# A layer-norm's inverse root seeded by one ScalarE operation, and its scaled tables built on GpSimd, ahead of a spectral filter and a GLU block

## The chip, the cores and the metric

The kernel runs on one core of a Trainium2 chip. The metric is device time of one execution in microseconds, as the median over runs of the same program. The core has a matrix engine (PE, TensorE; its weight loads are listed as PEld), VectorE (DVE), ScalarE (ACT), GpSimd (POOL), and SyncE (SP), whose queue issues most of the transfers.

## The reference

All tensors are fp32. S = 2048 rows, D = 640 columns, F = 1728.

```python
x = A_x                                            # (1, 2048, 640)
n = (x - mean(x, -1)) / sqrt(var(x, -1) + 1e-5)    # layer norm without weights
X = rfft2(n, axes=(-2, -1)) * (w_r + 1j * w_i)
h = x + irfft2(X, s=(S, D))
m = (h - mean(h, -1)) / sqrt(var(h, -1) + 1e-5)
out = h + ((m @ w_gate) * (m @ w_up)) @ w_down
```

## The kernel before, in words

Both transforms are written as matrix products. The 2048 rows are taken as 16 tiles of 128 rows (`NT = 16`; tile t holds every sixteenth row from t on), each in a buffer `x` of 128 partitions and 640 columns. The program has a first stage that takes the tiles one after the other, a second stage over 16 groups of frequencies (filter), the way back, a second norm, and then the GLU block, which takes some three quarters of the time. The order on every engine is the order in which the code records the operations; each engine works its own list in that order and waits on semaphores for what others produce.

**The first stage, a tile t.** The norm is never written out. Its mean goes into the folding, its scale into a table:

- *Statistics.* For some tiles DVE computes them (two `bn_stats` halves and a `bn_aggr`: lines 176, 179, 180, result `mv`), for others ACT (an `Identity` pass that sums the row, line 195, and a `Square` pass that sums the squares into `sq`, line 196). `m2` is twice the mean (line 182), `ve` the variance plus epsilon (lines 183 and 198).
- *Inverse root* (`inverse_root`, lines 205 to 209). ACT takes the square root `sd` of `ve`, DVE its reciprocal `r`, and three small DVE operations (`w`, `w`, `r`) make one Newton step. This is done in groups of tiles: 0, 1, (2,3), (4,5), (6 to 9), (10,11), (12,13), (14,15).
- *Scaled table* (`scale_c`, lines 267 and 269). `CR[t]` is a 128 x 128 table `cct` whose rows are multiplied by `r`. It lies in one of four buffers (in `bits`). The list `SCALE_ON_ACT` says which engine makes it: ACT for tiles 0 and 5 to 15, DVE for tiles 1 to 4.
- *Folding* into one of four buffers `fold`: `odd` (line 229, on DVE, or on POOL for the tiles named in `FOLDS` and for tile 0) is a two-input subtraction of 320 columns; `even` is a two-input operation with the mean (line 234, 322 columns) and two further two-input sums (lines 238 and 239, 64 and 320 columns).
- *Product* (`s1_mm`, line 252): seven matrix products against `CR[t]`, each run as two fp32 passes, 14 passes a tile. The first four products need only the results of lines 234 and 229, the last three also those of lines 238 and 239.
- ACT copies the results out of PSUM (`s1_main`, line 278, and `s1_rest`, line 275).

On POOL, ahead of the `odd` of another tile, stands a one-element copy `hold` (line 360) that reads the last folding of the tile before: it keeps POOL from starting earlier.

`weave` and the list in `GROUPS` put the small operations of the inverse root between the big ones on DVE. `scale_shift` uses the same `moments` and `inverse_root` for the second norm, in four groups.

Of the kernel before, what the change touches and what calls it, by code (L numbers as in the profile page):

```python
# [37 lines left out]
SCALE_ON_ACT = (0, *range(AHEAD, NT))  # L38
# [40 lines left out]
def tile_spectral_glu(ctx: ExitStack, tc: tile.TileContext, x, wre, wim, wgu, wlast, wdown, wdlast,  # L79
                      cc, ci, fmain, frem, imain, irem, mm, out):  # L80
    nc = tc.nc

    keep = ctx.enter_context(tc.tile_pool(name="keep", bufs=1))
    work = ctx.enter_context(tc.tile_pool(name="work", bufs=8))
    small = ctx.enter_context(tc.tile_pool(name="small", bufs=5))
# [3 lines left out]
    tt, act = nc.vector.tensor_tensor, nc.scalar.activation  # L89
# [10 lines left out]
    def bank(tag, bufs=2):  # L100
        return pools["y" if tag in ("im2", "ir2") else "a"].tile([P, 512], F32, tag=tag, name=tag, bufs=bufs)
# [28 lines left out]
    cct = keep.tile([P, P], F32, name="cct")  # L130
# [34 lines left out]
    def moments(ts, junk=None, total=None, k=0):  # L165
        n = len(ts)
        m2 = small.tile([P, n], F32, tag="m2", name="m2")
        ve = small.tile([P, n], F32, tag="ve", name="ve")

        def statistics(ts):  # L170
            n = len(ts)
            mv = small.tile([P, n, 2], F32, tag="mv", name="mv")
            fs, late = [], None
            for i, t in enumerate(ts):
                st = small.tile([P, 2, 6], F32, tag="st", name="st")
                fs.append(lambda st=st, t=t: nc.vector.bn_stats(st[:, 0], X[t][:, 0:320]))
                if late:
                    fs.append(late)
                fs.append(lambda st=st, t=t: nc.vector.bn_stats(st[:, 1], X[t][:, 320:640]))
                late = lambda st=st, i=i: nc.vector.bn_aggr(mv[:, i], st)  # L180
            fs.append(late)
            fs.append(lambda: nc.vector.tensor_scalar(m2[:, 0:n], mv[:, :, 0], 2.0, None, op0=OP.mult))
            fs.append(lambda: nc.vector.tensor_scalar(ve[:, 0:n], mv[:, :, 1], EPS, None, op0=OP.add))
            return fs

        if junk is None:
            return m2, ve, statistics(ts)
        first = statistics(ts[:k]) if k else []
        sq = small.tile([P, n], F32, tag="sq", name="sq")
        fs = []  # L190
        if total is not None:
            fs.append(lambda: nc.vector.tensor_scalar(m2, total, 2.0 / D, None, op0=OP.mult))
        for i, t in list(enumerate(ts))[k:]:
            if total is None:
                fs.append(lambda t=t, i=i: act(junk[i], X[t], AF.Identity, scale=2.0 / D, accum_out=m2[:, i:i + 1]))
            fs.append(lambda t=t, i=i: act(junk[i], X[t], AF.Square, bias=m2[:, i:i + 1], scale=-2.0,
                                           accum_out=sq[:, i:i + 1]))
        fs.append(lambda: nc.vector.tensor_scalar(ve[:, k:n], sq[:, k:n], 0.25 / D, EPS, op0=OP.mult, op1=OP.add))
        return m2, ve, first + fs

    def inverse_root(ve, r, n):
        sd = small.tile([P, n], F32, tag="sd", name="sd")
        w = small.tile([P, n], F32, tag="w", name="w")
        return [
            lambda: act(sd, ve, AF.Sqrt),
            lambda: nc.vector.reciprocal(r, sd),
            lambda: nc.vector.scalar_tensor_tensor(w, r, -0.5, r, op0=OP.mult, op1=OP.mult),  # L207
            lambda: tt(w, w, ve, op=OP.mult),
            lambda: nc.vector.scalar_tensor_tensor(r, w, 1.5, r, op0=OP.add, op1=OP.mult),
        ]  # L210

    SC = {}

    def front(ts, k):
        n = len(ts)
        r = small.tile([P, n], F32, tag="r", name="r")
        junk = [fold[:, o:o + D] for o in (NR * 1026, NR * 1026 + D)]
        m2, ve, fs = moments(ts, junk * 2 if k < n else None, k=k)
        for i, t in enumerate(ts):
            SC[t] = r[:, i:i + 1], m2[:, i:i + 1]  # L220
        return fs, inverse_root(ve, r, n)

    def folded(t):
        o = t % NR * 1026
# [18 lines left out]
    PS1, CR = {}, {}  # L243
# [19 lines left out]

    def scale_c(t):
        CR[t] = crs[t % 4]
        if t in SCALE_ON_ACT:
            act(CR[t], cct, AF.Copy, scale=SC[t][0])
        else:
            nc.vector.tensor_scalar(CR[t], cct, SC[t][0], None, op0=OP.mult)

    def at(base, t):
        return view(base, 4 * t, [[64, 32], [1, 4]])
# [17 lines left out]

    warm = wk([P, P], "warm")
    nc.vector.memset(warm, 0.0)
    pw = bank("re")
    for n in range(16):
        nc.tensor.matmul(pw[:, 0:P], warm, warm, start=True, stop=True)
    f0, c0 = front((0,), 1)
    f1, c1 = front((1,), 0)
    for f in f0:
        f()
    for ts, when, aside, root in GROUPS:  # L300
        k = len(when)
        fs, cs = front(ts, k)
# [15 lines left out]
    for t in range(NT):  # L318
        if t == 1:
            nc.gpsimd.dma_start(frall, frem)  # L320
        if t >= 1:
            fs = even(t)
            if t + 1 < NT and t + 1 not in ASIDE:
                fs.insert(1, (0.4, lambda: odd(t + 1, nc.vector)))
            if t < AHEAD:
                fs.insert(1 + (t <= 2), (0.2, lambda: scale_c(t)))
            if t == 1:
                fs, (recip, w, *left) = fs[1:], dve[1][0]
                for f in (c1[4], fs[0][1], fs[1][1], recip, fs[2][1], w):
# [24 lines left out]
        else:  # L354
            e0 = [f for _, f in even(0)]
            c0[0]()
            for f in (e0[0], c0[1], e0[1], c0[2], c0[3], e0[2], c0[4], *f1[:-1]):
                f()
        if t in FOLDS:
            nc.gpsimd.tensor_copy(small.tile([P, 1], F32, tag="hold", name="hold"), folded(t)[1][:, 383:384])  # L360
            for k in FOLDS[t]:
                odd(k, nc.gpsimd)
        if t >= 1:
            for f in stats[t]:
                f()
            if AHEAD <= t + 1 < NT and t + 1 not in SCALE_ON_ACT:
                scale_c(t + 1)
        else:
            scale_c(0)
# [378 lines left out]
    def scale_shift(ts, junk, total=None):  # L748
        n = len(ts)
        r = small.tile([P, n], F32, tag="r", name="r")  # L750
        b = small.tile([P, n], F32, tag="b", name="b")
        m2, ve, fs = moments(ts, junk, total)
        cs = inverse_root(ve, r, n)
# [105 lines left out]
    total = small.tile([P, 8], F32, tag="total", name="total", bufs=1)  # L859
# [310 lines left out]
    for n, (blk, p) in enumerate(steps):  # L1170
        if p == 6:
# [356 lines left out]
```

## Time and profile before

| | us |
|---|---|
| runs of the kernel | 674.58, 674.81, 676.47; median 674.81 |
| the profiled execution | 675.71, of which the span of the program 673.9 |
| PE busy in the span | 662.8 (98%) |
| DVE busy in the span | 471.3 (70%) |
| first product of the first stage starts | 8.97 after the span's start |
| first product of the second stage starts | 38.92 |
| PE waiting in between, by the window from 8.97 to 38.87 | 2.6 (27.29 busy of 29.90) |

Busy times of a whole span are averages over stages with different limits. A row of the timeline reads: start, duration, engine, line, operation, output<-inputs, shape, count, and in brackets how long the engine had been idle and what by the profile ended that. Rows of one engine overlap by some 0.08 us, since the next operation is set up while the last one drains.

### The profile page before, as it was taken

The numbers are of one execution on the slowest core, as the hardware profiler recorded it, in microseconds if no ns is written. First come the engines' busy times: TensorE is split into PE (matmuls) and PEld (weight loads), VectorE is DVE, ScalarE is ACT, GpSimd is POOL, SyncE is SP. The second block draws the span as 40 slices with busy tenths as digits, with TensorE's granted clock in tenths as the row PEclk, the third lists the DMA queues.
The fourth block names the chain that finished last, engine by engine and source line by source line (L and its number), as shares of the span: only waits on it lengthen the run. The fifth ranks groups of instructions, "written<-read, shape, count | busy, mean of one in ns | idle before, by whom it ended". The sixth has DMA issues, their size and how long they took to land.

```text
span 673.9 us, 10264 instructions
## 1 busy us (share of the span) xinstructions
PE 662.8 (98%) x3695; PEld 588.0 (87%) x3695; DVE 471.3 (70%) x967; ACT 322.7 (48%) x622; POOL 393.0 (58%) x377
## 2 busy tenths in 40 slices
PE   7999999999999999999999999999999999999997
PEld 6999898887898888888888899898888888888887
DVE  6969896788767868584858657754747575756654
ACT  6977674585624244362626246534434252525220
POOL 3101124650298887878787544188787878787610
PEclk9999999999999999999999999999999999999999
DMA  8638975502212110042342458212002121212004
GB/s 317 225 103 258 268 223 157 179 6 78 79 40 78 40 59 25 36 115 63 92 84 79 98 116 274 79 40 68 16 34 79 40 78 40 79 40 80 1 1 156
DMA packets 48953, 66.12 MB, mean 98 GB/s; under 512 B 24082, under 2 KB 30670, under 8 KB 48774
## 3 DMA queue, kind: packets, MB, share of 16 engines
q1 hardware_dynamic: 48246, 62.91, 30.6%
q0 software_dynamic: 288, 2.16, 0.8%
q8 instruction: 29, 0.48, 0.3%
q10 hardware_dynamic: 368, 0.39, 0.3%
q14 instruction: 22, 0.18, 0.1%
HBM read 54.61 MB, written 10.84 MB: 97 GB/s over the span
## 4 chain that ended last, share of the span: by engine, by line
PE 92%; DMA 4%; DVE 2%; issue 1%; ACT 1%; SPq 0%; DVEq 0%; ACTq 0%
PE e L119 49%; PE d L119 26%; PE eo L119 4%; PE re L119 2%; PE u L455 2%; PE y L119 2%; PE im L119 2%; PE im L507 2%; DMA x<-in_x_dram 2%; PE im L252 1%; DMA bits<-in_mm_dram 1%; PE ir L507 1%; DMA wts<-in_wre_dram 1%; PE y L773 0%; SPq L155 0%
## 5 line engine op out<-in xcount | busy, mean ns | idle before, releaser
L119 PE MATMUL e<-xt,wst 128*128 128x512 f32 x864 | 213.2, 391 | 0.0
L119 PEld LDWEIGHTS e<-xt,wst 128*128 128x128 f32 x864 | 159.9, 188 | 30.5
L1047 DVE TENSOR_TENSOR x<-d,x 128x320 f32<-128x320 f32 x280 | 123.3, 483 | 51.6 <-PE d L119 47.6
L119 PE MATMUL d<-wd,ht 128*128 128x320 f32 x832 | 143.6, 309 | 0.0
L119 PEld LDWEIGHTS d<-wd,ht 128*128 128x128 f32 x832 | 131.2, 188 | 7.6
L961 POOL TENSOR_TENSOR wst<-raw,wst 128x1024 fp32r<-128x1024 f32 x23 | 55.4, 2409 | 67.2 <-ACT wst L960 49.2
L119 PE MATMUL e<-t,wst 128*128 128x512 f32 x360 | 94.4, 392 | 0.0
L119 PEld LDWEIGHTS e<-t,wst 128*128 128x128 f32 x360 | 66.3, 188 | 12.6
L119 PE MATMUL d<-wt,ht 128*128 128x320 f32 x360 | 69.5, 310 | 0.0
L977 POOL TENSOR_TENSOR wst<-raw,wst 128x896 fp32r<-128x896 f32 (+1 forms) x46 | 65.1, 1438 | 0.2 <-ACT wst L972 0.2
L119 PEld LDWEIGHTS d<-wt,ht 128*128 128x128 f32 x360 | 57.3, 188 | 2.3
L1063 ACT ACTIVATE ht<-e 128x512 fp32r<-128x512 f32 x44 | 26.4, 599 | 51.5 <-DVE e L1126 25.9
L1102 ACT ACTIVATE h<-e 128x512 f32<-128x512 f32 x24 | 14.3, 595 | 67.3 <-PE e L119 67.3
L1022 DVE TENSOR_TENSOR x<-d,x 128x320 f32<-128x320 f32 x62 | 27.5, 485 | 23.4 <-PE d L119 23.4
L658 ACT ACTIVATE wd<-draw 128x320 fp32r<-128x320 f32 (+1 forms) x30 | 15.7, 558 | 57.4 <-POOL draw L668 54.3
L972 ACT ACTIVATE wst<-raw 128x896 fp32r<-128x896 f32 (+1 forms) x48 | 30.2, 677 | 26.6 <-POOL raw L966 25.8
L119 PE MATMUL e<-xt,wdir 128*128 128x512 f32 x180 | 41.9, 392 | 0.4 <-DVE w L207 0.2
L119 PEld LDWEIGHTS e<-xt,wdir 128*128 128x128 f32 x180 | 33.5, 188 | 8.1 <-ACT xt L783 0.7
L1122 DVE TENSOR_TENSOR e<-e,h 128x512 f32<-128x512 f32 x24 | 16.8, 698 | 30.8 <-PE e L119 17.7
L1066 DVE TENSOR_TENSOR ht<-e,ht 128x512 fp32r<-128x512 f32 x54 | 36.9, 685 | 1.6 <-ACT ht L1063 1.3
L637 POOL TENSOR_TENSOR wd<-draw,wd 128x640 fp32r<-128x640 f32 x8 | 12.4, 1576 | 40.5 <-ACT wd L636 40.5
L1119 ACT ACTIVATE h<-e 128x512 f32<-128x512 f32 x24 | 14.3, 597 | 40.1 <-PE e L119 40.1
(234 smaller groups left out, 1189.5 us busy)
## 6 DMA issues: line engine op xcount, KB each, us to landing
raw<-in_wgu_dram SPq DMA_DIRECT2D x24, 640.0 KB
draw<-in_wdown_dram SPq DMA_DIRECT2D x24, 320.0 KB
wts<-in_wre_dram SPq DMA_DIRECT2D x16, 322.0 KB
x<-in_x_dram SPq DMA_DIRECT2D x15, 320.5 KB
out_dram<-x SPq DMA_DIRECT2D x15, 320.0 KB
bits<-in_mm_dram SPq DMA_DIRECT2D x32, 128.0 KB
wts<-in_wim_dram SPq DMA_DIRECT2D x9, 322.0 KB
zfar<-zr SPq DMA_DIRECT2D x32, 80.0 KB
```

The lines of the kernel that those rows point to most:

```text
L119: nc.tensor.matmul(o, l, r, start=start, stop=stop, skip_group_check=True)
L507: nc.tensor.matmul(out, y[:, h, a:b], inv(g, h), start=n == 0, stop=n == len(ys) - 1)
L658: act(o[:, 0, a:a + n], src, AF.Copy)
L961: ptt(wa[:, 1], stage[:, 0:1024], f32(wa[:, 0]), op=OP.subtract)
L972: act(ws[:, 0, o:o + b - a], stage[:, a:b], AF.Copy)
L977: ptt(ws[:, 1, o:o + b - a], stage[:, a:b], f32(ws[:, 0, o:o + b - a]), op=OP.subtract)
L1022: tt(xv, ps[b][:, 0:320], xv, op=OP.add)
L1047: tt(xv, o, xv, op=OP.add)
L1063: act(hop[:, a, 0], src, AF.Copy)
L1066: engine.tensor_tensor(hop[:, a, 1], src, f32(hop[:, a, 0]), op=OP.subtract)
L1102: act(h0, oa, AF.Copy)
L1122: tt(ob, ob, h1, op=OP.add)
```

## The change

Four things are changed in the first stage, and the first of them in the second norm too, which calls the same functions.

1. The square root on ACT and the reciprocal on DVE become one ACT operation, `Abs_reciprocal_sqrt`, whose result is the seed `r`. Where a group's variance comes from one engine alone, it reads the variance `mv` or the sums `sq` directly, with epsilon as a bias (a new 128 x 1 constant `eps`), and where it comes from `bn_aggr` alone, the addition of epsilon (`ve`) goes too: the Newton step adds it itself.
2. The scaled tables of tiles 3 to 15 are made by POOL: eleven leave ACT, two (tiles 3 and 4) leave DVE. Tiles 1 and 2 stay on DVE, tile 0 on ACT. On POOL a table stands where `t` is one less than its tile, ahead of the `hold` and `odd` of that `t`.
3. Tile 0's table stands between the two passes of tile 1's statistics on ACT, where it stood behind both.
4. On DVE, the last folding of tile 0 (line 239) stands behind the end of tile 0's Newton step, where it stood ahead of it.

The diff, without the second norm's call sites:

```diff
-        return m2, ve, statistics(ts)
-        first = statistics(ts[:k]) if k else []
+            fs = statistics(ts, True)
+            var = spread_of["mv"]
+            return m2, (var, 1.0, lambda w: nc.vector.scalar_tensor_tensor(w, var, EPS, w, op0=OP.add, op1=OP.mult)), fs
+        first = statistics(ts[:k], False) if k else []
...
-        return m2, ve, first + fs
+        times = lambda w: tt(w, w, ve, op=OP.mult)
+        return m2, ((ve, None, times) if k else (sq, 0.25 / D, times)), first + fs
...
-    def inverse_root(ve, r, n):
-        sd = small.tile([P, n], F32, tag="sd", name="sd")
+    def inverse_root(spread, r, n):
+        src, scale, times = spread
         w = small.tile([P, n], F32, tag="w", name="w")
+        root = AF.Abs_reciprocal_sqrt
         return [
-            lambda: act(sd, ve, AF.Sqrt),
-            lambda: nc.vector.reciprocal(r, sd),
+            lambda: act(r, src, root) if scale is None else act(r, src, root, bias=eps, scale=scale),
+            lambda: None,
             lambda: nc.vector.scalar_tensor_tensor(w, r, -0.5, r, op0=OP.mult, op1=OP.mult),
-            lambda: tt(w, w, ve, op=OP.mult),
+            lambda: times(w),
             lambda: nc.vector.scalar_tensor_tensor(r, w, 1.5, r, op0=OP.add, op1=OP.mult),
         ]
...
     def scale_c(t):
         CR[t] = crs[t % 4]
-        if t in SCALE_ON_ACT:
+        if t == 0:
             act(CR[t], cct, AF.Copy, scale=SC[t][0])
         else:
-            nc.vector.tensor_scalar(CR[t], cct, SC[t][0], None, op0=OP.mult)
+            (nc.vector if t < 3 else nc.gpsimd).tensor_scalar(CR[t], cct, SC[t][0], None, op0=OP.mult)
...
+    eps = keep.tile([P, 1], F32, name="eps")
+    nc.vector.memset(eps, EPS)
...
-            if t < AHEAD:
+            if t < 3:
                 fs.insert(1 + (t <= 2), (0.2, lambda: scale_c(t)))
...
-                if t + 1 in SCALE_ON_ACT:
-                    scale_c(t + 1)
...
-            for f in (e0[0], c0[1], e0[1], c0[2], c0[3], e0[2], c0[4], *f1[:-1]):
+            for f in (e0[0], c0[2], e0[1], f1[0], c0[3], c0[4]):
                 f()
+            scale_c(0)
+            for f in (e0[2], f1[1]):
+                f()
+        if 3 <= t + 1 < NT:
+            scale_c(t + 1)
```

What this does to the order is shown at three places. On POOL, from the `hold` of tile 1 to the end of the first stage, before (`hold` and the foldings of tiles 3, 4, 9 and 11):

```order
L360 COPY hold<-fold 128x1
L229 TENSOR_TENSOR fold<-x_71 128x2x160
L360 COPY hold<-fold 128x1
L229 TENSOR_TENSOR fold<-x_72 128x2x160
L360 COPY hold<-fold 128x1
L229 TENSOR_TENSOR fold<-x_77 128x2x160
L360 COPY hold<-fold 128x1
L229 TENSOR_TENSOR fold<-x_79 128x2x160
```

The same stretch of POOL now, with the thirteen tables (`bits`) in it:

```order
L379 COPY hold<-fold 128x1
L243 TENSOR_TENSOR fold<-x_71 128x2x160
L283 TENSOR_SCALAR bits<-cct,r 128x128
L379 COPY hold<-fold 128x1
L243 TENSOR_TENSOR fold<-x_72 128x2x160
L283 TENSOR_SCALAR bits<-cct,r 128x128 x5
L379 COPY hold<-fold 128x1
L243 TENSOR_TENSOR fold<-x_77 128x2x160
L283 TENSOR_SCALAR bits<-cct,r 128x128 x2
L379 COPY hold<-fold 128x1
L243 TENSOR_TENSOR fold<-x_79 128x2x160
L283 TENSOR_SCALAR bits<-cct,r 128x128 x5
```

The table of tile 3 comes ahead of the folding of tile 4, those of tiles 4 to 8 ahead of the folding of tile 9, those of 9 and 10 ahead of the folding of tile 11, and the last five end POOL's part of the stage.

ACT from its one table load on, before (x_69 is tile 1, x_72 tile 4):

```order
L205 ACT_TABLE_LOAD
L205 ACTIVATE sd<-ve 128x1
L195 ACTIVATE fold,m_146<-x_69 128x640
L196 ACTIVATE fold,sq<-x_69,m_146 128x640
L267 ACTIVATE bits<-cct,r 128x128
L195 ACTIVATE fold,m_165<-x_72 128x640
```

ACT from the same place now:

```order
L219 ACT_TABLE_LOAD
L219 ACTIVATE r<-mv,eps 128x1
L207 ACTIVATE fold,m_146<-x_69 128x640
L281 ACTIVATE bits<-cct,r 128x128
L208 ACTIVATE fold,sq<-x_69,m_146 128x640
L207 ACTIVATE fold,m_161<-x_72 128x640
```

Tile 0's table (`bits`) has moved ahead of the second pass over tile 1; there is still one table load, at the same place.

DVE around the middle of tiles 3 and 4, before (x_71 is tile 3, x_72 tile 4):

```order
L234 SCALAR_TENSOR_TENSOR fold<-x_71,m_157 128x2x161
L206 RECIPROCAL r<-sd 128x2
L180 BN_AGGR mv<-st 128x2
L269 TENSOR_SCALAR bits<-cct,r 128x128
L207 SCALAR_TENSOR_TENSOR w<-r 128x2
L182 TENSOR_SCALAR m_171<-mv 128x2
L238 TENSOR_TENSOR fold<-fold 128x64
L208 TENSOR_TENSOR w<-w,ve 128x2
L183 TENSOR_SCALAR ve<-mv 128x2
L239 TENSOR_TENSOR fold<-fold 128x2x160
L209 SCALAR_TENSOR_TENSOR r<-w,r 128x2
L234 SCALAR_TENSOR_TENSOR fold<-x_72,m_165 128x2x161
```

DVE over the same stretch now:

```order
L248 SCALAR_TENSOR_TENSOR fold<-x_71,m_155 128x2x161
L184 BN_AGGR mv<-st 128x2
L252 TENSOR_TENSOR fold<-fold 128x64
L221 SCALAR_TENSOR_TENSOR w<-r 128x2
L186 TENSOR_SCALAR m_166<-mv 128x2
L253 TENSOR_TENSOR fold<-fold 128x2x160
L211 TENSOR_TENSOR w<-w,ve 128x2
L192 TENSOR_SCALAR ve<-mv 128x2
L223 SCALAR_TENSOR_TENSOR r<-w,r 128x2
L248 SCALAR_TENSOR_TENSOR fold<-x_72,m_161 128x2x161
```

The reciprocal and tile 3's table are gone from it, and the rest stands in nearly the same order.

More of the change, by code (lines that the diff above doesn't have):

```diff
@@ L37 @@
 TURNS = {6: ((0, 1), (1, 2), (2, 3)), 8: ((3, 1), (4, 2), (5, 3)), 10: ((6, 1), (7, 2))}
-SCALE_ON_ACT = (0, *range(AHEAD, NT))
 GROUPS = (((2, 3), (0, 0), (), 1), ((4, 5), (), (0, 0, 1, 1), 3), ((6, 7, 8, 9), (1, 2), (2, 2, 3, 3), 5),
@@ L167, in moments, with wide, statistics @@
         m2 = small.tile([P, n], F32, tag="m2", name="m2")
-        ve = small.tile([P, n], F32, tag="ve", name="ve")
-        def statistics(ts):
+        spread_of = {}
+        def wide():
+            if "ve" not in spread_of:
+                spread_of["ve"] = small.tile([P, n], F32, tag="ve", name="ve")
+            return spread_of["ve"]
+        def statistics(ts, alone):
             n = len(ts)
@@ L182, in statistics @@
             fs.append(lambda: nc.vector.tensor_scalar(m2[:, 0:n], mv[:, :, 0], 2.0, None, op0=OP.mult))
-            fs.append(lambda: nc.vector.tensor_scalar(ve[:, 0:n], mv[:, :, 1], EPS, None, op0=OP.add))
-            return fs
-        if junk is None:
-            return m2, ve, statistics(ts)
-        first = statistics(ts[:k]) if k else []
+            if alone:
+                spread_of["mv"] = mv[:, :, 1]
+                fs.append(lambda: None)
+            else:
+                ve = wide()
+                fs.append(lambda: nc.vector.tensor_scalar(ve[:, 0:n], mv[:, :, 1], EPS, None, op0=OP.add))
+            return fs
+        if junk is None or k == n:
+            fs = statistics(ts, True)
+            var = spread_of["mv"]
+            return m2, (var, 1.0, lambda w: nc.vector.scalar_tensor_tensor(w, var, EPS, w, op0=OP.add, op1=OP.mult)), fs
+        first = statistics(ts[:k], False) if k else []
         sq = small.tile([P, n], F32, tag="sq", name="sq")
+        ve = wide()
         fs = []
@@ L217, in front @@
         junk = [fold[:, o:o + D] for o in (NR * 1026, NR * 1026 + D)]
-        m2, ve, fs = moments(ts, junk * 2 if k < n else None, k=k)
+        m2, spread, fs = moments(ts, junk * 2 if k < n else None, k=k)
         for i, t in enumerate(ts):
             SC[t] = r[:, i:i + 1], m2[:, i:i + 1]
-        return fs, inverse_root(ve, r, n)
+        return fs, inverse_root(spread, r, n)
     def folded(t):
@@ L365, in tile_spectral_glu @@
                 f()
-            if AHEAD <= t + 1 < NT and t + 1 not in SCALE_ON_ACT:
-                scale_c(t + 1)
         else:
-            scale_c(0)
             b2a, b2, b3a, a2, b3, a3, m, v = stats[0]
@@ L751, in scale_shift @@
         b = small.tile([P, n], F32, tag="b", name="b")
-        m2, ve, fs = moments(ts, junk, total)
-        cs = inverse_root(ve, r, n)
+        m2, spread, fs = moments(ts, junk, total)
+        cs = inverse_root(spread, r, n)
         cs.append(lambda: nc.vector.scalar_tensor_tensor(b, m2, -0.5, r, op0=OP.mult, op1=OP.mult))
```

## The prediction

> **What bounds the kernel now.** I read the page first, then the windows of the first stage, then its timeline engine by engine.
>
> ```profile
> span 673.9 us, 10264 instructions
> PE 662.8 (98%) x3695; PEld 588.0 (87%) x3695; DVE 471.3 (70%) x967; ACT 322.7 (48%) x622; POOL 393.0 (58%) x377
> ```
>
> PE is busy in 98% of the span, so a change can win only where PE stands still, and it loses whatever makes PE stand longer. Windows of the first stage (columns: length, busy time of PE, PEld, DVE, ACT and POOL with instructions, granted clock, DMA share, GB/s):
>
> ```profile
> 8.97:38.87 29.90, 27.29 (x224) 26.21 (x225) 28.05 (x114) 27.17 (x81) 5.84 (x11) 1.00 0.65 239
> ...
> 15.00:20.00 5.00, 4.68 (x41) 4.52 (x40) 5.00 (x26) 4.82 (x15) 0.60 (x1) 1.00 1.03 400
> 20.00:25.00 5.00, 4.89 (x42) 4.67 (x41) 4.90 (x15) 5.00 (x16) 1.00 (x2) 1.00 1.06 370
> ...
> 29.10:38.90 9.80, 9.76 (x84) 9.77 (x85) 8.24 (x33) 7.77 (x24) 0.00 (x0) 1.00 0.06 15
> ```
>
> PE stands 29.90 - 27.29 = 2.6 us in the stage, all of it before 29.1: from there PE paces itself. Until then DVE and ACT are both full, so which of them does PE wait for? The timeline, with tiles 8, 10 and 15:
>
> ```profile
> 23.55 0.86 POOL L229 TENSOR_TENSOR fold<-x 128x320 f32<-128x320 f32 x1
> 23.66 0.47 DVE L179 BATCH_NORM_STATS2 st<-x 128x6 f32<-128x320 f32 x1
> ...
> 24.06 0.70 DVE L234 SCALAR_TENSOR_TENSOR fold<-x,m 128x322 f32<-128x322 f32 x1
> 24.10 0.45 ACT L267 ACTIVATE bits<-cct,r 128x128 f32<-128x128 f32 x1
> ...
> 24.87 2.56 PEld L252 LDWEIGHTS im<-bits,fold 128*128 128x128 f32 x22 [0.27 <-ACT bits L267]
> ...
> 28.36 0.63 DVE L234 SCALAR_TENSOR_TENSOR fold<-x,m 128x322 f32<-128x322 f32 x1
> 29.14 3.19 PE L252 MATMUL im<-bits,fold 128*128 128x128 f32 x26 [0.54 <-DVE mv L180]
> ...
> 35.63 2.57 PEld L252 LDWEIGHTS im<-bits,fold 128*128 128x128 f32 x22
> 36.29 0.54 DVE L234 SCALAR_TENSOR_TENSOR fold<-x,m 128x322 f32<-128x322 f32 x1
> ```
>
> The bracket names ACT at 24.87, but that table was done at 24.55, and DVE's folding ends at 24.76: PE starts 0.11 behind DVE. So too at 29.14: the folding of tile 10 ends at 28.99. PE waits for foldings, and DVE folds without a pause, so in the front part a microsecond of DVE work is a microsecond of PE. At the end there is slack. The 22 passes from 35.63 on are tile 14's fourteen and tile 15's first eight, at 2.57 / 22 = 0.117 each, so tile 15 is due at 35.63 + 14 x 0.117 = 37.27, and its folding is there at 36.83. With 0.1 for the signal that leaves 0.34.
>
> **The change, part by part: tile 0.** DVE's rows, and what hangs on them:
>
> ```profile
> 6.50 0.15 DVE L182 TENSOR_SCALAR m<-mv 128x1 f32<-128x1 f32 x1
> 6.57 0.14 DVE L183 TENSOR_SCALAR ve<-mv 128x1 f32<-128x1 f32 x1
> ...
> 6.77 0.55 DVE L234 SCALAR_TENSOR_TENSOR fold<-x,m 128x322 f32<-128x322 f32 x1
> ...
> 7.24 0.15 DVE L206 RECIPROCAL r<-sd 128x1 f32<-128x1 f32 x1
> ...
> 8.17 0.15 DVE L209 SCALAR_TENSOR_TENSOR r<-w,r 128x1 f32<-128x1 f32 x1
> 8.24 0.49 DVE L176 BATCH_NORM_STATS2 st<-x 128x6 f32<-128x320 f32 x1
> ...
> 8.53 0.39 ACT L267 ACTIVATE bits<-cct,r 128x128 f32<-128x128 f32 x1
> ...
> 8.97 1.67 PEld L252 LDWEIGHTS im<-bits,fold 128*128 128x128 f32 x14 [2.22 <-ACT bits L267]
> 11.71 1.44 PEld L252 LDWEIGHTS im<-bits,fold 128*128 128x128 f32 x12 [1.07 <-issue]
> ```
>
> Without `ve` the folding starts at 6.70, without the reciprocal and with the big sum put last `r` is there at about 7.8 instead of 8.32, and the table, no longer behind the second ACT pass, at 8.2 instead of 8.92. PE begins some 0.7 earlier. That is worth nothing by itself: tile 1 starts at 11.71 whatever tile 0 does, long after tile 0's 1.67. What counts is when DVE gets to the next statistics: 0.07 earlier by `ve`, and 0.06 of the reciprocal's step, the rest of which goes into waiting for the folding, so 0.13. Tile 1's seed now stands on ACT behind a pass over tile 4 (the second row below is where DVE uses the seed):
> ```profile
> 8.82 0.72 ACT L195 ACTIVATE fold<-x 128x640 f32<-128x640 f32 x1
> ...
> 10.72 0.15 DVE L207 SCALAR_TENSOR_TENSOR w<-r 128x1 f32<-128x1 f32 x1
> ```
>
> That pass starts 0.2 later; with 0.72, 0.2 for its accumulator and 0.2 for the seed it is done at 10.1, and DVE asks at 10.6: covered. The new constant `eps` is set before DVE's first input lands: nothing.
>
> **The reciprocals and the tables that leave DVE.** A removed operation is worth the step from its start to the next start:
>
> ```profile
> 17.56 0.28 DVE L269 TENSOR_SCALAR bits<-cct,r 128x128 f32<-128x128 f32 x1
> 17.75 0.48 DVE L229 TENSOR_TENSOR fold<-x 128x320 f32<-128x320 f32 x1
> ...
> 19.23 0.17 DVE L206 RECIPROCAL r<-sd 128x4 f32<-128x4 f32 x1
> 19.32 0.46 DVE L229 TENSOR_TENSOR fold<-x 128x320 f32<-128x320 f32 x1
> ```
>
> That is 0.19 for a table and 0.09 for a reciprocal. Up to tile 10 fall two tables (0.19 + about 0.15 for tile 3's, which stands beside waits) and four reciprocals of 0.07 to 0.09, together 0.65; tile 1's I count at nothing, since its neighbours wait for each other and fill the place. With tile 0's 0.13 that is 0.78. From tile 11 to 15 go two more reciprocals and one `ve`, at 0.08, 0.08 and 0.07: 1.01 by tile 15.
>
> **The tables that leave ACT.**
>
> ```profile
> L267 ACT ACTIVATE bits<-cct,r 128x128 f32<-128x128 f32 x12 | 5.0, 418 | 0.3 <-DVE r L209 0.3
> ```
>
> Eleven times 0.42 is 4.6 us of ACT. I cost it at nothing, since PE waited for DVE at each stop above; it is the second rival.
>
> **The thirteen tables on POOL** are what the sum hangs on. POOL has time (5.84 of 29.90), but it stands in DVE's way, and the quoted rows show it. The folding of line 234 takes 0.54 or 0.55 when POOL is idle. At 24.06 it takes 0.70, and ends 0.35 after POOL's operation (23.55 + 0.86 = 24.41); at 28.36 it takes 0.63. The statistics at 23.66 ran through the same POOL operation in their usual 0.47. So an operation of DVE with two inputs waits until POOL is done, and then needs 0.35; the statistics don't wait. The other way round, and what a short POOL operation takes:
>
> ```profile
> 112.41 0.50 DVE L725 TENSOR_TENSOR yt<-q 128x322 f32<-128x322 f32 x1
> 112.46 1.05 POOL L733 TENSOR_TENSOR yt<-q 128x318 f32<-128x318 f32 x1 [2.17 <-DVE q L729]
> ...
> 130.81 0.75 POOL L733 TENSOR_TENSOR yt<-q 128x318 f32<-128x318 f32 x1
> ...
> L536 POOL CAST qr<-bits 1x128 fp32r<-1x128 f32 x15 | 4.2, 279 | 45.7 <-DVE qr L540 45.7
> L537 POOL TENSOR_TENSOR qr<-bits,qr 1x128 fp32r<-1x128 f32 x15 | 6.7, 450 | 1.2
> ```
>
> POOL loses 0.30 behind a DVE operation that has 0.45 left: the first 0.15 of a POOL operation run beside DVE. No row shows a table on POOL. The nearest is the one-input cast of 128 elements at 0.28; the two-input one at 0.45 is the upper neighbour. Of the 0.28, then, 0.13 come after DVE's end. DVE's next 320-column sum by itself would have got going 0.05 after it (0.48, less the 0.35 that it needs, less the 0.08 of overlap), so a table costs DVE 0.08; the pointer to `r` is in neither row, and I take 0.12. The ends are 0 (all tables fall beside statistics) and 0.45 - 0.05 = 0.40 (a two-input length, and nothing of it beside DVE).
>
> The Trainium skill (SBUF — State Buffer, section Who interferes with whom) says that a DVE instruction with two SBUF inputs and a GpSimd instruction that reads SBUF shut each other out for the whole instruction, the first to start winning. The trace agrees that they exclude each other, with 24.41 + 0.35 = 24.76; it shows a smaller loss, 0.30 and not 0.45. By the page's whole instruction a table would cost 0.28 - 0.05 = 0.23 and the sum below would be 1.3 higher.
>
> Where do they fall? By the order, tile 3's table runs when its `r` is done, during two-input work; 4 to 8 likewise; 9 right behind the folding of tile 9 on POOL; 10 beside the statistics, but it pushes the folding of tile 11 back by 0.12, and DVE's folding of tile 10, which waits for that; 11 to 15 again beside two-input work. That is 7 prices and 0.12 up to tile 10, 12 and 0.12 up to tile 15. The tables themselves are in time: POOL can be three tiles ahead, except for 10, 12 and 14, whose `r` comes just before.
>
> **The sum.** At tile 10: 7 x 0.12 + 0.12 - 0.78 = +0.18. At tile 15: 12 x 0.12 + 0.12 - 1.01 = +0.55, less the slack of 0.34, +0.21. Both say that the second stage starts 0.2 later. Behind it PE works on without long waits, so that goes through to the end. The second norm loses four reciprocals, of which PE saw at most one:
>
> ```profile
> 153.35 3.69 PE L119 MATMUL e<-xt,wdir 128*128 128x512 f32 x15 [0.24 <-DVE w L207]
> ```
>
> Up to 0.1 is won there. In all +0.1: 675.8 against the profiled execution's 675.71 (its span is 673.9, and 1.8 lie around it), which is 0.9 above the median of the three runs; against the median of 674.81 it is 674.9. A measurement tells some 0.3% (2.0 us) from no change, and this is far inside.
>
> **The rivals.**
> - *The tables cost DVE nothing.* The statistics at 23.66 speak for it, the folding at 24.06 against. Then tile 10 is won by 0.78, with the second norm 0.9: 673.9. From tile 10 on PE paces itself, so there is no more in it.
> - *ACT was the limit.* The windows speak for it (5.00 of 5.00 from 20 to 25) and the releasers in the brackets; against it that DVE's folding ended last at both stops. If ACT's delays were in DVE's chain unseen, nearly all of PE's 2.6 could go, and then tile 0's 0.7 as well: at half of the 3.3, 673.2, at most 671.5.
> - *POOL holds DVE longer.* The 0.45 row and the missing pointer speak for it. With price c the stage grows by 12c + 0.12 - 1.01 - 0.34. At 0.25 that is +1.8, or 676.5 with the second norm's 0.1; it becomes slower by more than 2.0 from c = 0.28 on, and at 0.40 it is +3.6, or 678.3.
> - *The tables come late.* DVE's two-input sums stand back to back, and POOL might find no gap between them. The first row below is tile 14's `r`, the second the last sum of its folding:
>
> ```profile
> 34.81 0.15 DVE L209 SCALAR_TENSOR_TENSOR r<-w,r 128x2 f32<-128x2 f32 x1
> ...
> 35.88 0.48 DVE L239 TENSOR_TENSOR fold<-fold 128x320 f32<-128x320 f32 x1
> ```
>
> If POOL gets its turn only at 36.36, the table is there at 36.5, 0.8 behind the 35.63 at which PE took up tile 14. Three times that (tiles 10, 12 and 14) is 2.4: 677.2. Against it: at 112.46 POOL got in as soon as one operation had ended.
>
> **How the numbers follow.** The forecast (674.0 to 676.2) gets 0.54, the free tables 0.16, ACT as the limit 0.12, the longer hold 0.12, late tables 0.06. The range of 8 in 10 leaves out the ends of ACT's case and of the longer hold: 672.8 to 677.0. Faster by over 2.0 is about two thirds of ACT's case, 0.08; slower is half of the longer hold and most of the late tables, 0.11; the rest, 0.81, is no change.
>
> **What would show it.** In the profile after: PE's first product at about 8.2, tile 1's still near 11.6; the tables on POOL at 0.28 to 0.35, stretched to 0.4 or 0.5 where DVE is at work; more of DVE's foldings and sums at 0.55 to 0.65 in place of 0.48; ACT's share of the stage down by 4 us without PE gaining it; the first product of the second stage between 38.5 and 39.5 in place of 38.92. Wrong would be a PE without stops from 14 us on (ACT was the limit), brackets at PE that name POOL's tables (late tables), or tables of 0.45 and more without a wait (the longer hold).

## The result, and the profile after

The changed kernel takes 679.93 us (median of 9 runs, 679.36 to 681.63); the kernel before, run beside it, 675.84 (9 runs). The ratio is 1.0059, with a 95% interval of 1.0041 to 1.0077: slower by 4.1 us, where no change was forecast. The profiled execution took 679.69, with a span of 677.9 at a granted clock of 0.999, so it may be held against the 673.9 of before. The windows of the first stage, cut at the same places as before (length, busy PE, PEld, DVE, ACT, POOL, granted clock, DMA share, GB/s):

```profile
8.40:42.05 33.65, 27.52 (x224) 26.11 (x225) 28.58 (x104) 26.00 (x72) 21.27 (x25) 1.00 0.59 220
15.00:20.00 5.00, 4.29 (x35) 3.93 (x35) 5.00 (x21) 4.90 (x14) 2.70 (x4) 1.00 1.04 403
20.00:25.00 5.00, 3.27 (x29) 3.08 (x28) 4.90 (x17) 3.05 (x8) 4.24 (x3) 1.00 1.06 371
29.10:42.00 12.90, 11.43 (x97) 10.89 (x95) 9.90 (x34) 8.09 (x23) 7.68 (x8) 1.00 0.04 12
```

PE now stands 33.65 - 27.52 = 6.1 us in the stage, against 2.6. From 20 to 25 us it is busy 3.27 of 5.00, where it was busy 4.89; DVE is as full as before, ACT no longer is (it waits for PE's results in order to copy them). And POOL is busy for 21.27 us with 25 instructions, against 5.84 with 11. The groups of POOL in the stage say why (mean ns in the last number ahead of the second bar):

```profile
L283 POOL TENSOR_SCALAR bits<-cct,r 128x128 f32<-128x128 f32 x13 | 14.8, 1144 | 8.7 <-DVE r L223 5.0 <-PE im L266 3.6
```

A table lasts 1.14 us in the mean, where 0.28 to 0.5 had been foretold. PE's timeline from tile 4 on (tiles 4, 6, 10, 12 and 14 begin at the brackets):

```profile
18.67 3.22 PE L266 MATMUL im<-bits,fold 128*128 128x128 f32 x26 [0.43 <-POOL bits L283]
...
23.85 3.23 PE L266 MATMUL im<-bits,fold 128*128 128x128 f32 x26 [1.73 <-POOL bits L283]
...
30.98 3.19 PE L266 MATMUL im<-bits,fold 128*128 128x128 f32 x26 [0.51 <-DVE mv L184]
...
35.20 3.22 PE L266 MATMUL im<-bits,fold 128*128 128x128 f32 x26 [0.80 <-POOL bits L283]
...
38.81 2.75 PE L266 MATMUL im<-bits,fold 128*128 128x128 f32 x22 [0.17 <-POOL bits L283]
...
42.10 0.34 PE L118 MATMUL im<-tab,s 128*128 128x160 f32 x1
```

Four of the five brackets name POOL's tables, and the second stage's first product comes at 42.10 instead of 38.92. What holds up the tables is seen when POOL and DVE are read side by side. First POOL, then DVE:

```profile
20.76 4.37 POOL L283 TENSOR_SCALAR bits<-cct,r 128x128 f32<-128x128 f32 x3 [1.43 <-DVE r L223]
...
26.23 0.60 POOL L283 TENSOR_SCALAR bits<-cct,r 128x128 f32<-128x128 f32 x1
...
33.45 2.59 POOL L283 TENSOR_SCALAR bits<-cct,r 128x128 f32<-128x128 f32 x2 [2.14 <-DVE r L223]
36.69 2.88 POOL L283 TENSOR_SCALAR bits<-cct,r 128x128 f32<-128x128 f32 x2 [0.65 <-DVE r L223]
```

```profile
20.45 0.15 DVE L223 SCALAR_TENSOR_TENSOR r<-w,r 128x4 f32<-128x4 f32 x1
20.52 0.54 DVE L248 SCALAR_TENSOR_TENSOR fold<-x,m 128x322 f32<-128x322 f32 x1
20.98 0.48 DVE L243 TENSOR_TENSOR fold<-x 128x320 f32<-128x320 f32 x1
21.38 0.21 DVE L252 TENSOR_TENSOR fold<-fold 128x64 f32<-128x64 f32 x1
...
22.92 0.48 DVE L253 TENSOR_TENSOR fold<-fold 128x320 f32<-128x320 f32 x1
23.32 0.48 DVE L180 BATCH_NORM_STATS2 st<-x 128x6 f32<-128x320 f32 x1
...
27.12 0.17 DVE L210 TENSOR_SCALAR ve<-sq 128x2 f32<-128x2 f32 x1 [1.74 <-ACT fold L208]
```

The first of the three tables in the 4.37 us (tiles 6, 7 and 8) begins at 20.76 and ends at 23.79, 3.03 us for what takes 0.60 at 26.23, where DVE stands still. Between 20.52 and 23.41 DVE runs eight two-input operations, each in its usual time and each started 0.08 before the end of the one ahead, and POOL gets nothing. It gets its turn when the statistics begin. The last row is the echo: PE was late, so ACT's copy was late (2.1 us at 25.52), and so were the `Square` pass queued behind it and DVE's `ve`.

The stage accounts for 3.2 of the 4.0 us by which the spans differ. The rest is further on. I followed the starts of PE's weight loads, of which both kernels have the same 3695. From the 450th to the 520th, where one wait stands, the changed kernel takes 9.92 us and the kernel before 10.94. From the 1200th (at 196.7 and 194.5 us) to the 3600th, where PE never waits long, it takes 463.53 against 461.72. So 3.2 - 1.0 + 1.8 = 4.0. Windows of 200 us in the GLU block show the last term as a count of products, first before, then after:

```profile
450.00:650.00 200.00, 200.00 (x1041) 175.96 (x1040) 122.80 (x239) 77.48 (x130) 152.06 (x134) 1.00 0.15 50
```

```profile
450.00:650.00 200.00, 200.00 (x1038) 175.40 (x1037) 123.22 (x239) 75.89 (x127) 153.30 (x133) 1.00 0.14 50
```

Three products fewer at a granted clock of 1.00 in both. That part lies far behind anything the change touches.

### The profile page after: what moved, and what is told of

The parts are those of the page before. It is cut to its first block, busy times and chain, and to the rows that moved or that the text cites. A ratio compares the mean times of both kernels' runs of the same rounds, so it can differ in the third digit from the quotient of the medians.

```text
span 677.9 us, 10260 instructions
## 1 busy us (share of the span) xinstructions
PE 664.0 (98%) x3695; PEld 587.4 (87%) x3695; DVE 471.1 (69%) x950; ACT 321.2 (47%) x611; POOL 408.4 (60%) x390
## 4 chain that ended last, share of the span: by engine, by line
PE 91%; DMA 4%; DVE 3%; ACT 1%; issue 1%; POOL 0%; SPq 0%; POOLq 0%; DVEq 0%; ACTq 0%
PE e L118 49%; PE d L118 26%; PE eo L118 4%; PE re L118 2%; DMA bits<-in_mm_dram 2%; PE u L471 2%; PE y L118 2%; PE im L118 2%; PE im L523 2%; DMA x<-in_x_dram 2%; PE ir L523 1%; PE im L266 0%; DVE fold L248 0%; PE y L789 0%; POOL bits L283 0%
## 5 line engine op out<-in xcount | busy, mean ns | idle before, releaser
L1118 ACT ACTIVATE h<-e 128x512 f32<-128x512 f32 x24 | 14.3, 596 | 68.0 <-PE e L118 68.0
L1038 DVE TENSOR_TENSOR x<-d,x 128x320 f32<-128x320 f32 x62 | 27.5, 485 | 23.1 <-PE d L118 23.1
L266 PE MATMUL im<-bits,fold 128*128 128x128 f32 x204 | 25.6, 281 | 8.2 <-POOL bits L283 3.1
```

The lines of the kernel that those rows point to most:

```text
L266: nc.tensor.matmul(o, l, c, start=n == 0, stop=n == len(ls) - 1)
L1038: tt(xv, ps[b][:, 0:320], xv, op=OP.add)
```

## The experiments

"Stage" below is the start of the second stage's first product (its weight load), "GLU" the time from the 1200th to the 3600th weight load, "450 to 520" the stretch with the one wait. These three come from one profiled execution of each kernel; medians and ratios are against the kernel before on the same chip.

| kernel | stage | 450 to 520 | GLU | median | before | ratio, 95% |
|---|---|---|---|---|---|---|
| before, first profile | 38.86 | 10.94 | 461.72 | | | |
| changed kernel | 42.04 | 9.92 | 463.53 | 679.93 | 675.84 | 1.0041 to 1.0077 |
| e0_before_again | 38.73 | 10.46 | 461.73 | 675.63 | 675.66 | 0.9983 to 1.0017 |
| e1_seed_only | 38.31 | 11.15 | 463.81 | 677.25 | 675.66 | 1.0004 to 1.0045 |
| e2_tables_only | 43.39 | 10.14 | 461.70 | 681.07 | 675.66 | 1.0051 to 1.0098 |
| e4_seed_small | 38.17 | 11.31 | 461.75 | 675.58 | 675.87 | 0.9977 to 1.0014 |
| e5_pad32 | 38.79 | 9.92 | 463.51 | 676.65 | 675.87 | 1.0006 to 1.0036 |
| e6_seed_pad64 | 38.24 | 10.33 | 463.23 | 676.38 | 675.87 | 0.9999 to 1.0024 |
| e8_pauses | 40.07 | 9.92 | 461.73 | 676.95 | 675.93 | 0.9999 to 1.0036 |
| e9_after_small | 41.95 | 10.75 | 462.02 | 678.56 | 675.93 | 1.0021 to 1.0056 |
| e10_pad_ring | 39.17 | 10.44 | 461.76 | 675.86 | 675.93 | 0.9973 to 1.0015 |
| e11_seed_pad128 | 38.20 | 10.05 | 462.59 | 675.28 | 675.93 | 0.9980 to 1.0013 |
| e12_pad_between | 38.67 | 11.27 | 462.82 | 676.53 | 675.67 | 1.0004 to 1.0041 |

A part of the column "stage" is the landing of the first input. DVE's first statistics, which wait for it, start between 5.05 us (e4, the first row) and 5.63 (e10, the second):

```profile
5.05 0.49 DVE L181 BATCH_NORM_STATS2 st<-x 128x6 f32<-128x320 f32 x1 [4.04 <-DMA x<-in_x_dram]
```

```profile
5.63 0.49 DVE L176 BATCH_NORM_STATS2 st<-x 128x6 f32<-128x320 f32 x1 [4.62 <-DMA x<-in_x_dram]
```

Counted from them, the second stage starts after 33.52 to 33.56 us in the five profiles with the old seeds and tables (both of the kernel before, e5, e10, e12), after 33.12 to 33.14 in the four with the seeds alone (e1, e4, e6, e11), after 36.63 and 36.60 in the changed kernel and e9, and after 34.69 in e8. So the seeds win 0.40, and beside them the tables on POOL lose 3.5.

**The same kernel again.** No edit.

> The kernel before, unchanged, profiled a second time on the chip of the other runs. The profiles of before and after part by +3.2 us up to the second stage, fall back to +2.1 at 76 us, and then drift apart from 188 us on, evenly, by 0.4% of the time, to +4.0 at the end. If that drift belongs to the execution or the chip (PE a little slower in one of them), this second profile of the same program drifts against the first one by up to 2 us from 188 us on, with nothing moved before it; if it belongs to the change, this profile lies on the first within 0.3 us everywhere. The time is the same within 0.3% by both.

It measured 675.63. GLU time is the same to 0.01 us, so a difference of 1.8 there is no scatter of executions. The wait between the 450th and 520th load does scatter: 0.5 us between two profiles of one program.

**The change in two halves.** The seeds and tile 0's order, with the tables given back to ACT and DVE:

```diff
-        if t == 0:
+        if t in SCALE_ON_ACT:
             act(CR[t], cct, AF.Copy, scale=SC[t][0])
         else:
-            (nc.vector if t < 3 else nc.gpsimd).tensor_scalar(...)
+            nc.vector.tensor_scalar(...)
```

> The change without its tables: one ScalarE operation as the seed and tile 0's table between the passes, but the tables of tiles 3 and 4 on DVE and those of 5 to 15 on ACT as before. Theory of late tables (POOL's tables wait for the port behind DVE's two-input operations, and PE waits for them): no wait of PE on a POOL table, the second stage starts at 38.3 to 38.9 (before 38.9, after 42.1), and the time is 0 to 1 us below before. Rival (the seeds or tile 0's new order cost the time): the second stage starts at 40 or later and the time is 2 us or more above before.

And the kernel before with the tables of tiles 3 to 15 on POOL, old seeds:

```diff
-SCALE_ON_ACT = (0, *range(AHEAD, NT))
+SCALE_ON_ACT = (0,)
...
+        if 3 <= t + 1 < NT:
+            scale_c(t + 1)          # on nc.gpsimd
```

> The kernel before with nothing changed but the tables of tiles 3 to 15, which POOL makes at the places where the changed kernel has them; square root and reciprocal as before. Late tables: PE waits for POOL tables near tiles 4, 6, 12 and 14, 2 to 4 us in all, the second stage starts at 41.5 to 42.5, and the time is 2 to 4.5 us above before, as with the whole change. Rival (the seeds cost the time): the second stage starts within 0.7 of before's 38.9.

The tables alone make the stage late (43.39), the seeds alone make it 0.4 to 0.55 earlier (38.31). So the late tables are the stage's loss. All runs of e2 had a granted clock of 0.946 to 0.997 (in its profile 0.82 from 8 to 20 us). PE is busy for 29.1 us with the 224 table products of its stage, where before has 27.5, so up to 1.6 of the 4.5 us may be the clock's, and its median can't be split. The surprise was e1: it wins in the stage and still ends at 677.25, since its GLU time is 2.1 longer. The second loss goes with the seeds' half of the change, and with GLU products that the seeds don't touch.

**POOL and DVE alone (the port measurement).** A kernel in which DVE and POOL alone work: POOL makes a 128 x 128 table while DVE runs a chain of equal operations.

> Not the computation: x is copied to the output, and ahead of that ten short phases run, in each of which POOL gets one operation (a 128 x 128 table with a pointer scalar; in phase 8 a two-input 320-column one) that becomes ready as DVE starts a chain. 0: no chain. 1: eight two-input sums of 320 columns. 2 to 4: two of them, then a one-element memset (2), a statistics operation (3) or a sum that needs the one before it (4), then six more. 5: ten one-input scalings. 6: eight sums with one input in PSUM. 7: ten two-input sums of 64 columns. 8: as 1, against the two-input POOL operation. 9: four two-input sums. Theory (POOL gets the port only when DVE leaves a gap or runs something that doesn't use it): the table takes 0.6 us in 0 and 6, some 3.5 in 1 (the whole chain of 8 x 0.40), about 1.4 in 3 and 4, and 2.0 in 9. Rival (POOL gets in behind whatever operation is running, as I predicted): 0.6 to 1.0 in all phases, and DVE's next sum takes 0.2 to 0.3 more.

POOL's timeline:

```profile
4.89 0.60 POOL L50 TENSOR_SCALAR tab<-cct,r 128x128 f32<-128x128 f32 x1 [4.47 <-DVE r L47]
5.78 1.10 POOL L50 TENSOR_SCALAR tab<-cct,r 128x128 f32<-128x128 f32 x1 [0.29 <-DVE r L47]
...
20.09 2.73 POOL L50 TENSOR_SCALAR tab<-cct,r 128x128 f32<-128x128 f32 x1 [2.68 <-DVE r L47]
23.11 0.60 POOL L50 TENSOR_SCALAR tab<-cct,r 128x128 f32<-128x128 f32 x1 [0.29 <-DVE r L47]
...
27.87 3.19 POOL L53 TENSOR_TENSOR pf<-r,cct 128x2 f32<-128x2 f32 x1 [0.81 <-DVE r L47]
```

In turn: alone 0.60; beside eight two-input sums 1.10; beside ten one-input scalings 2.73, until the chain had ended; beside sums with one input in PSUM 0.60. Not shown: beside ten 64-column sums 0.70, beside four two-input sums 1.09, and with a one-element memset, a statistics operation or a dependent sum behind the second sum 1.51, 1.18 and 1.18. The last row is another operation of POOL, two columns wide with two inputs, and it too waited out all eight sums. My theory (POOL gets in only at a gap; 3.5 expected beside eight sums, 2.0 beside four) did not hold for the tables: the one at 5.78 got in after the second sum, which then cost the third 0.10. So I repeated it with the kernel's own forms.

> DVE and POOL alone (the input goes to the output unchanged; the rest is left out), as in the first port measurement, where a table of 128 columns on POOL took 0.60 us alone, 1.1 through eight equal sums of plain rows, and 2.7 (the whole chain) through one-input scalings. Now through the kernel's own forms: twice folding, odd sum, 64-column sum, 320-column sum (phases 1 and 8); eight foldings; eight odd sums with a reversed row; eight 320-column sums with every second column written; the same with a statistics in the middle; plain rows of 322, 64 and 320 columns three times; ten plain sums. Theory 'form': a folding or a reversed or strided sum leaves POOL no gap, so phases 1, 8 and at least one of the three pure phases last the whole chain (2.7 to 3.3 us) while the plain ones stay near 1.1, and the phase with statistics ends inside the statistics, 1.9 to 2.2 after its start. Rival 'mixture': the pure phases all end near 1.1, and only mixed lengths starve POOL, the plain mixture too. Rival 'something else in the kernel' (ScalarE, PE or transfers): every phase near 1.1.

POOL's rows for the kernel's sequence and for eight odd sums, then DVE's rows beside the first:

```profile
10.00 1.16 POOL L50 TENSOR_SCALAR tab<-cct,r 128x128 f32<-128x128 f32 x1 [0.94 <-DVE r L47]
...
17.92 0.78 POOL L50 TENSOR_SCALAR tab<-cct,r 128x128 f32<-128x128 f32 x1 [3.83 <-DVE r L47]
```

```profile
9.82 0.55 DVE L78 SCALAR_TENSOR_TENSOR f<-xp,m 128x322 f32<-128x322 f32 x1
10.29 0.48 DVE L81 TENSOR_TENSOR f<-xp 128x320 f32<-128x320 f32 x1
10.81 0.23 DVE L83 TENSOR_TENSOR j<-f 128x64 f32<-128x64 f32 x1
10.95 0.48 DVE L84 TENSOR_TENSOR j<-f 128x320 f32<-128x320 f32 x1
```

No phase lasted longer than 1.16. That does not rule out "form" or "mixture", for the start times show that these chains have pauses, which the kernel's stretch does not have. Here the operations of a chain write the same buffers and wait for each other: the folding starts at 9.82 and the odd sum at 10.29, before the folding's end, but the 64-column sum starts at 10.81, 0.04 after the odd sum's end at 10.77. At that first pause POOL gets in: 10.77 + 0.39 = 11.16. So too in seven of the other eight phases (18.23 + 0.47 = 18.70); the table at 8.29 got in at a seam, the boundary of two operations without a pause. In the changed kernel nothing waits between 20.52 and 23.41, and there are no pauses. At a seam without a pause POOL was passed over 7 times at 20.76, 4 times at 36.69 and 7 times at 27.87 in the port measurement, and got in at a few others (by their ends less 0.39, at 6.49 there and at 18.23 in the changed kernel), each time holding up the operation behind. What singles these out the runs do not show, so whether the forms of the operations have a part in it stays open.

The Trainium skill (SBUF — State Buffer, Who interferes with whom) lets the engine that issues first have the shared ports for a whole instruction, and says that DVE scalings can need them too. The 2.73 us agree with the second; the first the 3.03 us contradict, since the table's row starts at 20.76, ahead of seven of the eight operations that it waited for.

**Giving POOL a pause, in the kernel.** First the whole change with `eps` in the pool of small tiles (the reason follows below), then the same with DVE's odd sum of the next tile ahead of the folding, so that the 64-column sum waits for the folding directly:

```diff
-    eps = keep.tile([P, 1], F32, name="eps")
+    eps = small.tile([P, 1], F32, tag="eps", name="eps", bufs=1)
```

> The whole change, with eps in the pool of small tiles, so that nothing large moves. If two causes add up (late tables 3.2 us in the first stage, and 1.8 to 2.0 us of slower products behind 190 us by the 32 bytes), then the first stage stays as late as in the changed kernel (second stage's first product at 42.1) and the falling back goes: 678.0 where the changed kernel had 679.9 and the kernel before 675.8. If the layout only mattered with the old tables: 679.9.

It measured 678.56: the stage is as late as in the changed kernel, and GLU time falls back to within 0.3 of the kernel before (no run says where the 0.3 comes from). The two losses add up, as expected.

```diff
-                fs.insert(1, (0.4, lambda: odd(t + 1, nc.vector)))
+                fs.insert(0 if t >= 3 else 1, (0.4, lambda: odd(t + 1, nc.vector)))
```

> As the whole change with eps in the small pool, but from tile 3 on DVE takes the next tile's odd sum ahead of the folding instead of behind it. The 64-column sum then follows directly on the folding that it reads, and DVE pauses between the two (0.03 us from the end of one to the start of the next in the port measurement, against an overlap of 0.08 where nothing is waited for). Theory 'POOL gets in at a pause': no table lasts above 1.4 us (0.55 + 0.48 for the two sums ahead of the pause, and 0.39 from there), PE's waits for tables shrink from 3.9 + 3.1 us to under 2, DVE pays some 0.11 in each of nine tiles, and the second stage's first product comes at 39.5 to 40.5 instead of 42.1: time 676 to 676.5. Rival 'POOL gets in by chance at any boundary': tables of 2 to 3 us stay, the stage is as late as before or later by the 1 us of pauses, 678 to 679.

POOL's group of tables, and its timeline, with pauses:

```profile
L283 POOL TENSOR_SCALAR bits<-cct,r 128x128 f32<-128x128 f32 x13 | 11.0, 852 | 10.3 <-DVE r L223 10.3
```

```profile
20.92 2.73 POOL L283 TENSOR_SCALAR bits<-cct,r 128x128 f32<-128x128 f32 x3 [2.15 <-DVE r L223]
...
32.35 1.81 POOL L283 TENSOR_SCALAR bits<-cct,r 128x128 f32<-128x128 f32 x2 [2.19 <-DVE r L223]
35.73 1.80 POOL L283 TENSOR_SCALAR bits<-cct,r 128x128 f32<-128x128 f32 x2 [1.57 <-DVE r L223]
```

The same operations in another order: no table lasts above 1.09 us, the stage starts at 40.07 instead of 41.95, and the median falls from 678.56 to 676.95 (676 to 676.5 had been expected). That shows the cause. Four of the seven tables in these rows got in at one of the new pauses (at 21.62, 23.18, 33.03 and 36.40), the other three at a seam. Counted from the first statistics, the stage is still 1.2 us later than before, and 1.6 later than with the seeds alone. The pauses, foreseen as 0.11 in each of nine tiles, come to 0.75 by their rows: 0.115 in five tiles, 0.04 in the four where a small operation stands between. The rest of the 1.6 is not taken apart.

**The second loss.** `eps` is the one thing in e1 that reaches the GLU block without being used there. It was allocated among the large tiles, takes 32 bytes with its padding, and so moves what is allocated behind it: the third GLU weight buffer (`wt`), an operand tile (`t3`), the ring of work tiles and the small ones. e4 is e1 with `eps` in the small pool; e5 is the kernel before with 32 unused bytes; e6 and e11 are e1 with `eps` 64 and 128 bytes wide.

```diff
+    pad = keep.tile([P, 8], F32, name="pad")    # e5: nothing else
+    nc.vector.memset(pad[:, 0:1], EPS)
```

> The kernel with the seeds and tile 0's order alone, but with the constant eps taken from the pool of small tiles (behind everything large) instead of standing between the large ones, where it pushed the GLU weights' third buffer and the ring of work tiles 32 bytes on. With eps among the large tiles, PE was 0.43 us ahead at 34.9 and 0.3 ahead at 190, and then fell back evenly, 0.4% of the time, to 1.8 behind at the end. Theory 'layout': the 32 bytes make PE's later products slower; then there is no falling back here, the first stage's win stays, and the time is 0.3 to 0.6 below the kernel before: 675.2 where that is 675.7. Rival 'the seed itself' (the new function on ScalarE, or one instruction less per tile): the falling back stays, time 677.3.

> The kernel before with nothing but an unused constant of 4 bytes (32 with its padding) at the place of eps, written once. Theory 'layout': the first stage as before, PE falls back evenly from 190 us on by 1.9 to 2.1 us, time 677.6 where the kernel before has 675.7. Rival 'the seed itself': 675.7, no change.

> The seeds and tile 0's order alone, with eps among the large tiles but 64 bytes wide, so that what lies behind it moves by 64 bytes and keeps its place modulo 64. Theory 'layout, modulo 64': no falling back, 675.2. Rival 'layout, any move': falling back of 2 us as with 32 bytes, 677.3. If the seed itself were the cause: 677.3 too, but then also with eps in the small pool.

> The seeds and tile 0's order alone, with eps 128 bytes wide among the large tiles. 32 and 64 bytes both cost 1.6 to 1.9 us behind 190 us. Theory 'place modulo 128': no slowing, 675.4. Rival 'any move': 1.6 to 2 us, 676.5 to 677.3.

The pad alone, in the kernel before, lengthens GLU time by 1.8 us, as much as the whole change does (463.51 and 463.53). Without it the seeds lose nothing (461.75). The products in the window, for e5 and for e4:

```profile
450.00:650.00 200.00, 200.00 (x1037) 175.33 (x1036) 122.49 (x238) 77.49 (x130) 151.34 (x134) 1.00 0.14 50
```

```profile
450.00:650.00 200.00, 200.00 (x1043) 175.92 (x1042) 123.11 (x240) 77.49 (x130) 152.03 (x133) 1.00 0.14 50
```

The place modulo 64 or 128 is not the rule: 64 bytes cost 1.5 and 128 bytes 0.9. (In the profiles of e5, e6 and e11 the wait between the 450th and the 520th load was short, which hides a part of that in the whole: e5's median is 0.8 above the kernel before, where 1.9 to 2.1 had been expected.) Then which tile? The pad behind all large tiles, and between the two last ones:

> The kernel before with an unused constant of 32 bytes behind the last of the large tiles, so that only the ring of work tiles (and the small ones behind it) moves, and no GLU weight buffer. Theory 'ring': the products slow down behind 190 us as with the pad further ahead (0.4%, 1.9 us at the end; 676.6 to 677.6). Rival 'third weights' buffer': no slowing, 675.8. The small tiles had moved without harm where eps stood among them.

> The kernel before with 32 unused bytes between the two last large tiles: the GLU weights' third buffer (wt, 7680 bytes) keeps its place, the operand tile t3 behind it (4096 bytes) and the ring move by 32 bytes. The ring alone had cost nothing, all three together 1.8 to 1.9 us behind 190 us. Theory 'wt': no slowing, 675.9. Rival 't3': slowing of 1.8 us, 676.6 to 677.7. Rival 'each a part': between the two.

Moving the ring and the small tiles costs nothing (461.76), `t3` with them 1.1 (462.82), `wt` as well 1.8. So each of the two has a part. The slower products are not only those that read the moved tiles: half of the 1.8 us that e5 loses (0.95) falls on the products of `xt` with `wst`, which both keep their places. By what mechanism the place of one tile slows these, no run here shows.

No version is measurably faster than the kernel before. The nearest of the kernels with the seeds are e4 and e11, without the tables, and their intervals hold 1.

## Why the prediction was wrong, step by step

- **Tile 0** was nearly right. PE's first product came at 8.40 (foretold 8.2, before 8.97), and nothing came of that by itself. Tile 1's came at 11.81, where 11.6 had been foretold: 6.37 behind the first statistics, by the starts of the weight loads, as before.
- **Removed reciprocals and `ve`** were right: the prediction's sum without its two tables is 0.44 by tile 10 and 0.67 by tile 15, and counted from the first statistics the seeds win 0.40 in the stage of e1, e4, e6 and e11.
- **The tables that leave ACT** were costed at nothing. ACT is busy for 3.05 us of the five from 20 on, where it was busy for 5.00, and PE gained nothing by it, as it then waited for POOL. No run takes the tables from ACT without a new wait elsewhere, so that ACT was no limit is not shown.
- **The price to DVE** (0.12 a table) had the right sign and was too high. In the changed kernel five operations that ran beside tables alone were slower, by 0.05 to 0.1 each. Where POOL waits, DVE pays nothing.
- **The length of a table** was taken from a cast of one partition, 0.28. A table takes 0.60 undisturbed. The two-input row at 0.45 was nearer, and served only as the upper end. By the prediction's own signs, tables of 0.45 and more without a wait would have meant the longer hold; they came, but DVE's loss did not.
- **"The tables themselves are in time"** is the step that failed. It rested on the row at 112.46, of which the prediction said that POOL got in as soon as one operation had ended. It did, but DVE's next row in the same view, which was not read, says why:

```profile
113.26 0.49 DVE L728 TENSOR_TENSOR q<-eo,s 128x322 f32<-128x322 f32 x1 [0.36 <-ACT s L720]
```

  From 112.91 DVE stood still and waited for ACT. The row at 112.46 shows POOL entering a pause and says nothing of back-to-back sums, of which the first stage is full. The mechanism was among the rivals, at a chance of 0.06 and a price of 2.4, and the sign by which it would be known (brackets that name POOL's tables) was right. It cost 3.5 in the stage, of which the seeds gave 0.4 back: it struck at tiles 4, 6, 12 and 14 instead of 10, 12 and 14, and the wait at tile 6 went round through ACT to DVE.
- **"That goes through to the end"** was half right: 1.0 of the 3.2 vanished in the wait near 76 us, whose length differs between profiles by up to 1.4.
- **The second norm** was right: its wait went from 0.24 to 0.18.
- **`eps`** was costed as one short instruction, "nothing". Its 32 bytes cost 1.8 us of GLU time, and 0.8 to 1.9 in the medians (e5; the changed kernel against e9; e1 against e4, each relative to its kernel before). No row of the profile before shows that; no term of the sum asked what a new allocation moves.

The late tables alone (678.56 in e9) leave the range, the 32 bytes alone (676.65 in e5) do not.

## What to carry to other kernels

Before work is moved to GpSimd beside a VectorE that runs two-input operations back to back, look for VectorE's pauses: in these runs GpSimd got in at every one of them while it waited, and a row that shows GpSimd "getting in" proves nothing until VectorE's next row has been read. A pause can be made by putting an operation directly behind the one that it reads; it cost VectorE 0.04 to 0.115 us here, and the nine together won 1.9. And put a new constant behind the large buffers or in a spare slot: compare addresses, not only instructions.

## What the runs showed of the hardware that was not expected

- A GpSimd operation can wait through eight two-input operations of VectorE (3.03 and 3.19 us) and through ten one-input scalings (2.73), while VectorE loses next to nothing. Beside statistics, or sums with one input in PSUM, it takes its 0.60 to 0.7.
- A start of 0.08 before the end of the operation ahead, or 0.03 to 0.04 behind it, tells a seam from a pause in VectorE's timeline, and only at the second did GpSimd get in every time.
- The place of two tiles in SBUF, moved by 32 bytes, changes TensorE's pace by 0.4% at a granted clock of 1.00, in the same way in each such kernel (GLU time 463.51, 463.53 and 463.81, against 461.70 to 462.02 in the seven profiles with both in place). Why is open.
